# An attention and MLP kernel: value products and MLP behind six runs of scores a chunk, read out by VectorE

## The chip, the cores and the metric

The kernel runs on one core of a Trainium2 chip. A core has TensorE (matrix products into PSUM), VectorE, ScalarE (activations such as the exponential), GpSimd and SyncE, whose queue issues most DMAs. Each engine works through its own list of instructions in order, and waits on semaphores for the others. In profiles they are PE (PEld for TensorE's weight loads), ACT, DVE, POOL and SP.

The metric is the device time of one execution in microseconds. A comparison of two kernels is made over several executions on the same chip.

## The reference

One input of 2048 tokens by 640 features goes through two blocks in parallel, and their sum is added to it.

```python
xn = _layernorm(x)
# attention: 32 heads of 20 features
qkv = (xn @ wqkv) -> q, k, v          # each 32 x 2048 x 20
p = softmax(q @ k.T * 20 ** -0.5)
o = p @ v
A = o.reshape(2048, 640) @ wo
# MLP with a layernorm of its own, 640 -> 1536 -> 640, tanh GELU
y = _layernorm(xn)
B = gelu(y @ w1 + b1) @ w2 + b2
out = x + A + B
```

All inputs and the output are fp32. The kernel keeps the precision by splitting operands into two 16-bit halves and summing three partial products (the table `PASS`), or by fp32 products.

## The kernel before, in words

The first stage (up to about 217 us) normalizes, projects to q, k and v (lines 345 and 418), and prepares the weights of the MLP. The second stage does the attention and, in between on TensorE, the MLP. The third, short one projects the attention's output (the tile `z`, line 1156).

In the attention stage heads go in 16 pairs `g`, queries in two halves `hf` of 1024, and each half in two column blocks `cc` of 512. One such triple is called a chunk here; there are 64. A chunk goes over the 2048 keys in 16 key blocks of 128. For each key block:

- `scores` makes two matmuls (one per head of the pair, in two row tiles of TensorE, line 758) into a PSUM tile `s`, of which there are three, and ScalarE's exponential (line 760) turns it into an SBUF tile `p`, of which there are seven.
- For key blocks marked 1 in `SPLIT`, `rest` has VectorE compute `low`, the tile `p` less its upper 16 bits (line 772). There are four such buffers.
- `pv` multiplies with the values (line 789), in four column tiles of 32. A split key block takes four matmuls with the upper halves and two with `low`; a whole one takes two fp32 products. All of a chunk's products go into one PSUM tile `o`, of which there is one. The row sums of the softmax come out of the same products, through a column of ones beside the values.

After the last key block the sums are copied to SBUF (`ev`, line 810, ScalarE) and, after a chunk with `cc` = 1, sent to DRAM (`unload`). `finish` later divides by the row sums, piece by piece, on VectorE.

The MLP is a Python generator, `chain()`. It yields the cost of what it has just issued, in microseconds, and is asked for more whenever the attention has credit for it. `layer1` makes `pu` (30 matmuls of 256 columns, line 1041), followed by `gelu` on VectorE with one tanh on ScalarE (line 987); `layer2` makes `py` (36 matmuls of 320 columns, line 1071), followed by `addup` (line 1007). Both use the one PSUM buffer `m`. When the MLP is through, the chain goes on with the output projection `z`, as far as the attention's results are there.

The order of all engines' instructions is written out by hand (`manual_schedule`): the last loop of the kernel. Before the change it takes key blocks in groups of four: two scores, some MLP, two scores, then the value products of the group before. `tick()` moves each side job (GELU steps, finishing, loads of the next pair, which go to SP's queue) one step on. `rate` and `credit` say how much of the chain goes into each slot, 1.265 us four times a chunk; `CHUNK` bounds a piece.

The lines that set the order, in the words of the kernel:

```python
SPLIT = (1, 1, 0, 0) * (NKB // 4)
GRP = 4
...
                            rest(units[0])
                            credit += rate
                            other()
                        else:
                            for u in units[1:]:
                                rest(u)
                            if prev:
                                pv(prev)
```

Of the kernel before, what the change touches and what calls it, by code (L numbers as in the profile page):

```python
# [9 lines left out]
F32 = mybir.dt.float32  # L10
F16 = mybir.dt.float16
# [7 lines left out]
P = 128  # L19
# [12 lines left out]
QS = float(DH) ** -0.5 / 4.0  # L32
KROW = 32768.0
GRP = 4
CHUNK = 1.75
UNITS = (3, 3, 3, 3, 2, 2)
ENDS = tuple(sum(UNITS[: i + 1]) for i in range(len(UNITS)))
TAIL = 12
# [6 lines left out]
def mha_mlp_kernel(tc, x, wqkv, wo, w1, b1, w2, b2, out):  # L45
# [4 lines left out]
    with (  # L50
# [31 lines left out]
        ones = keep.tile([P, P], F32, name="ones")  # L82
# [21 lines left out]
        def pow2(acc, tag, total=None):  # L104

            lo = keep.tile([P, 1], F32, name=f"lo_{tag}")
            hi = keep.tile([P, 1], F32, name=f"hi_{tag}")
            if total is None:
                if tag == "k":
                    pt = psM.tile([P, 512], F32, tag="m", name="mxp")  # L110
                else:
                    pt = psS.tile([P, 2, 512], F32, tag="s", name="mxp")[:, 0, :]
                n = acc.shape[1]
                nc.tensor.matmul(pt[:, :n], ones, acc, start=True, stop=True)
# [12 lines left out]
            whole(lo, hi)  # L127
            return lo, hi
# [2 lines left out]
            nc.vector.tensor_scalar(lo, lo, 2.0**64, None, ALU.mult)  # L131
            exponents(lo, hi)

        pw, scales = {}, {}

        def split(pool, src, h, l, scale, n):

# [36 lines left out]

        with tc.tile_pool(name="pa", bufs=2) as pa, tc.tile_pool(name="pa1", bufs=1) as pa1, tc.manual_schedule():
            wv = pa1.tile([P, KD, 3, 2, D], F16, name="wv")

            stage = {}
            for n, t, i in (("q", w1t, 0), ("v", w1t, 1), ("k", w2t, 0)):
# [15 lines left out]
            nhalf = keep.tile([P, 4], F32, name="nhalf")  # L195
            half = keep.tile([H, 1], F32, name="half")
            nc.gpsimd.memset(ones, 1.0)
            nc.gpsimd.memset(nhalf, -0.5)
            eps = keep.tile([P, 1], F32, name="eps")
            nc.gpsimd.memset(eps, EPS)  # L200
# [87 lines left out]
            def factors_out():  # L288

                pr = psM.tile([P, 512], F32, tag="m", name="pr")[:NKB, :P]  # L290
                nc.tensor.transpose(pr, rall, ident)
                rrow = sm.tile([NKB, P], F32, tag="rrow", name="rrow", bufs=1)
                nc.vector.tensor_copy(rrow, pr)
                nc.gpsimd.dma_start(rscr, rrow)

# [382 lines left out]
        with ExitStack() as scope:  # L678
            pool = lambda **kw: scope.enter_context(tc.tile_pool(reuse_waits="tile", **kw))
            m0 = pool(name="m0", bufs=2)  # L680
            m1 = pool(name="m1", bufs=1)
            ptp = pool(name="pt", bufs=2 * GRP - 1)

# [83 lines left out]
            def rest(unit):  # L767

                kb, pt = unit[3:]
                if SPLIT[kb]:  # L770
                    low = ptp.tile([P, 2, 512], F16, tag="low", name="low", bufs=GRP)
                    nc.vector.tensor_sub(low, pt, upper(pt))  # L772
                    unit.append(low)

            evs = {}

            def pv(units):

                g, hf, cc, kb0 = units[0][:4]
                if kb0 == 0:
                    pv.o = psO.tile([P, 512], F32, tag="o", name="o")
                    pv.begun = set()
                last = units[-1][3] == NKB - 1

                def product(q, src, v0, t):
                    nc.tensor.matmul(pv.o[32 * q : 32 * q + 32, :], src[:, v0 - PAD * (1 - q % 2) :][:, :32], t,  # L789
                                     start=q not in pv.begun, stop=last, skip_group_check=True)  # L790
                    pv.begun.add(q)

                split = [(u[3], upper(u[4]), u[5]) for u in units if SPLIT[u[3]]]
                whole = [(u[3], u[4]) for u in units if not SPLIT[u[3]]]
                of16 = lambda kb, a: 2 * PAD + kb * 2 * VROW + (2 * g + a) * 2 * VW
                of32 = lambda kb, a: PAD + kb * VROW + (2 * g + a) * VW
                for kb, up, _ in split:
                    for a in range(2):
                        product(2 * a, vhalf, of16(kb, a), up[:, a])
                        product(2 * a + 1, vhalf, of16(kb, a) + VW, up[:, a])  # L800
                for a in range(2):
                    for n, (kb, _, low) in enumerate(split):
                        product(2 * a + n % 2, vhalf, of16(kb, a), low[:, a])
                for a in range(2):
                    for n, (kb, pt) in enumerate(whole):
                        product(2 * a + n % 2, vfull, of32(kb, a), pt[:, a])
                if last:
                    if cc == 0:
                        evs[g, hf] = m1.tile([P, 2, 512], F32, tag="ev", name="ev")
                    nc.scalar.activation(evs[g, hf][:, cc], pv.o, AF.Copy)  # L810
                    if cc == 1:
                        unload(g, hf, evs.pop((g, hf)))

            def dma(g, hf):

# [55 lines left out]
            def finish(g0, g1, hf):  # L871
# [16 lines left out]
                for c0 in range(0, 1024, w):  # L888
# [297 lines left out]
            with tc.manual_schedule():  # L1186
                fill = chain()
                sides.append(fetch_sums())
                credit = 0.0 - next(fill)
                rate = 1.265  # L1190
                groups = [(g, hf, cc, kb) for g, hf in ORDER for cc in range(2) for kb in range(0, NKB, GRP)]
                prev = None

                runs = []

                def other():

                    nonlocal credit
                    if not runs:
                        unit = next(fill)  # L1200
                        if unit is None:
                            credit = 0.0
                            return
                        n, cost = unit
                        k = max(round((cost - credit) / rate) + 1, math.ceil(cost / CHUNK))
                        runs.extend(n * (i + 1) // k - n * i // k for i in range(k))
                    for _ in range(runs.pop(0)):
                        credit -= next(fill)

                for g, hf, cc, kb0 in groups:  # L1210
                    units = []
                    for kb in range(kb0, kb0 + GRP):
                        units.append([g, hf, cc, kb, scores(g, hf, cc, kb)])
                        if kb % 2 == 0:
                            continue
                        reading[0] = kb % GRP > 1 and prev is not None and prev[-1][3] == NKB - 1
                        tick()
                        if kb % GRP == 1:

                            rest(units[0])
                            credit += rate
                            other()
                        else:
                            for u in units[1:]:
                                rest(u)
                            if prev:
                                pv(prev)
                            else:  # L1230

                                credit += rate
                                other()
                    prev = units
                    if cc == 0 and kb0 == 0 and (g, hf) != ORDER[-1]:
                        n = ORDER[ORDER.index((g, hf)) + 1]
                        sides.append(load_stack(*n, *([stacks[g, hf][1]] if n[0] == g else [])))
                n = 0
                reading[0] = False
                ended[0] = True  # L1240
# [25 lines left out]
def general(tc, nc, V, vscr, qkscr, oscr, accscr, gscale, ident, psS, psO, psM, project):  # L1266
# [2 lines left out]
    ds = bass.ds  # L1269
    nc.sync.dma_start(vscr, V)  # L1270

    assert SPLIT == (1, 1, 0, 0) * (NKB // 4)
    with (
        tc.tile_pool(name="g2", bufs=2) as g2,
        tc.For_i(0, S, P) as t,
# [1 line left out]
        with tc.For_i(0, D, DH) as r:  # L1277
# [10 lines left out]
            for b in range(2):  # L1288
                nc.vector.tensor_add(vt[:, b::4, :], vp[:, b::4, :DH], vp[:, b::4, VW : VW + DH])
# [63 lines left out]
```

## Time and profile before

| | us |
|---|---|
| median of three runs | 1332.44 (1332.02 to 1332.53) |
| the profiled execution | 1332.15 |
| its span, first to last instruction | 1330.2 |
| TensorE busy | 1323.6 (100%) |
| ScalarE busy | 1128.5 (85%) |
| VectorE busy | 1055.4 (79%) |
| first score starts | 216.8 |
| last score starts | 1262.7 |

Some ways of writing need a word. `o<-p,vfull` is an instruction that writes tile `o` from `p` and `vfull`. A row of the timeline gives start, duration, engine, line, operation, shape and how many equal instructions are merged. TensorE's matmuls overlap: one that lasts 0.39 us may be followed by the next after 0.22, so a rate is read from starts and not from durations. A row of groups gives busy time, the mean in ns of one, and the engine's idle time just ahead of it with what ended it. The granted clock of TensorE was 0.999 of full over the span.

### The profile page before, as it was taken

How to read it: one execution, taken by the hardware profiler on the slowest of the kernel's cores; microseconds unless marked ns; L12 is line 12 of the kernel's file. 1: busy time of each engine (PE TensorE's matmuls, PEld its weight loads, DVE VectorE, ACT ScalarE, POOL GpSimd, SP SyncE). 2: the span in 40 equal slices, each digit the busy share in tenths (PEclk: the TensorE clock that was granted, in tenths of full speed). 3: DMA queues.
4: the chain of work that ended last, by engine and by line, in shares of the span. 5: the costliest groups of instructions: out<-in, count | busy, mean ns of one | idle time of the engine just before them, and what ended most of it. 6: DMA issues, size and time to landing. Idle time of an engine off the chain costs nothing.

```text
span 1330.2 us, 29036 instructions
## 1 busy us (share of the span) xinstructions
PE 1323.6 (100%) x11636; PEld 586.9 (44%) x11636; DVE 1055.4 (79%) x1432; ACT 1128.5 (85%) x1306; POOL 34.9 (3%) x83
## 2 busy tenths in 40 slices
PE   9999999999999999999999999999999999999998
PEld 6645546443434343434344444334443434333366
DVE  7657845998788888879887888888878888997742
ACT  7844425999999999999999999999999999999900
POOL 2000000000000000000000000000000000000000
PEclk9999999999999999999999999999999999999999
DMA  8765532111122323122322032323032323334375
GB/s 283 254 214 174 146 103 59 34 56 41 49 67 63 88 57 95 49 63 52 114 75 69 23 102 59 89 61 90 20 80 72 95 64 88 119 101 117 102 221 187
DMA packets 100230, 129.54 MB, mean 97 GB/s; under 512 B 24180, under 2 KB 66568, under 8 KB 100092
## 3 DMA queue, kind: packets, MB, share of 16 engines
q1 hardware_dynamic: 96652, 120.25, 30.1%
q0 software_dynamic: 2816, 6.90, 2.8%
q8 instruction: 92, 1.51, 0.5%
q10 hardware_dynamic: 624, 0.51, 0.1%
q14 instruction: 46, 0.38, 0.1%
HBM read 82.14 MB, written 42.51 MB: 94 GB/s over the span
## 4 chain that ended last, share of the span: by engine, by line
PE 95%; DVE 3%; ACT 1%; issue 0%; DVEq 0%; POOL 0%; ACTq 0%; POOLq 0%
PE o L789 30%; PE s L758 20%; PE pu L1041 12%; PE py L1071 12%; PE qkp L345 10%; PE z L1156 5%; PE vp L418 5%; DVE low L772 2%; PE warm L235 1%; ACT p L760 1%; PE norms L390 0%; DVE w1t L730 0%; PE rb L941 0%; DVE wtmp L725 0%; PE pt L307 0%
## 5 line engine op out<-in xcount | busy, mean ns | idle before, releaser
L760 ACT ACTIVATE p<-s 128x1024 f32<-128x1024 f32 x1024 | 973.7, 1048 | 33.1 <-PE s L758 27.3
L772 DVE TENSOR_TENSOR low<-p 128x1024 f16<-128x1024 f32 x512 | 614.9, 1219 | 144.5 <-ACT p L760 143.7
L789 PE MATMUL o<-p,vfull 128*32 128x512 bf16 (+1 forms) x4096 | 429.0, 493 | 0.0
L758 PE MATMUL s<-qs,ks 61*128 61x512 f16 x2048 | 311.4, 381 | 0.2 <-ACT p L760 0.2
L758 PEld LDWEIGHTS <-ks 61*128 61x128 f16 x2048 | 61.2, 94 | 278.4 <-issue 276.4
L1071 PE MATMUL py<-w2t,hT 128*128 128x320 f16 x1152 | 178.5, 300 | 0.1
L1041 PE MATMUL pu<-xm,w1t 128*128 128x256 f16 x1440 | 178.2, 273 | 0.1
L1041 PEld LDWEIGHTS <-w1t 128*128 128x128 f16 x1440 | 131.0, 98 | 64.0 <-issue 50.2
L1071 PEld LDWEIGHTS <-hT 128*128 128x128 f16 x1152 | 102.3, 98 | 88.2 <-issue 53.9
L345 PE MATMUL qkp<-xnt,wv 128*128 128x512 f16 x600 | 131.2, 379 | 0.0
L789 PEld LDWEIGHTS <-vfull 128*32 128x32 f16 x3072 | 59.9, 95 | 138.4 <-issue 106.9
L789 PE MATMUL o<-low,vfull 128*32 128x512 f16 x1024 | 101.3, 377 | 0.1
L345 PEld LDWEIGHTS <-wv 128*128 128x128 f16 x600 | 58.3, 98 | 69.4 <-DVE wv L459 1.0
L789 PEld LDWEIGHTS o<-p,vfull 128*32 128x32 f32 x2048 | 61.7, 108 | 53.1
L1156 PE MATMUL z<-w1t,ot 128*128 128x320 f16 x480 | 67.4, 299 | 0.0
L418 PE MATMUL vp<-wv,xnt 128*128 128x320 f16 x480 | 66.8, 299 | 0.0
L360 ACT ACTIVATE qkhl<-qkp,qks 128x1024 f16<-128x1024 f32 (+1 forms) x24 | 23.2, 967 | 48.6 <-PE qkp L345 35.9
L1156 PEld LDWEIGHTS <-ot 128*128 128x128 f16 x480 | 46.0, 98 | 22.9 <-issue 5.5
L418 PEld LDWEIGHTS <-xnt 128*128 128x128 f16 x480 | 46.7, 98 | 18.5
L361 DVE SCALAR_TENSOR_TENSOR qkhl<-qkp,qks,qkhl 128x1024 f16<-128x1024 f32 (+1 forms) x24 | 26.5, 1105 | 28.3 <-ACT qkhl L360 28.2
L1113 DVE SCALAR_TENSOR_TENSOR acc<-z,sc,acc 128x320 f32<-128x320 f32 x32 | 17.5, 549 | 38.4 <-PE z L1156 38.1
L810 ACT ACTIVATE ev<-o 128x512 f32<-128x512 f32 x64 | 39.4, 615 | 2.3 <-PE o L789 2.2
(198 smaller groups left out, 670.9 us busy)
## 6 DMA issues: line engine op xcount, KB each, us to landing
qkscr<-qkhl SPq DMA_DIRECT2D x40, 256.0 KB
opart<-ev SPq DMA_DIRECT2D x124, 80.0 KB
ks<-qkscr SPq DMA_DIRECT2D x120, 80.0 KB
qs<-qkscr SPq DMA_DIRECT2D x192, 40.0 KB
oa<-opart SPq DMA_DIRECT2D x32, 240.0 KB
xt<-in_A_x_dram SPq DMA_DIRECT2D x16, 320.0 KB
xscr<-xnt SPq DMA_DIRECT2D x4, 1280.0 KB
xm<-xscr SPq DMA_DIRECT2D x8, 640.0 KB
```

Of the source, the lines that this page charges most:

```text
L345: nc.tensor.matmul(ps[:, i, :], wv[:, k, q, a, mm * P : (mm + 1) * P], xnts[c][:, k, b, :], start=(k + n == 0), stop=(k == KD - 1 and n == 2))
L360: nc.scalar.activation(hl[:, 0, i0:i1], ps[:, i0:i1], AF.Copy, scale=a)
L361: nc.vector.scalar_tensor_tensor(hl[:, 1, i0:i1], ps[:, i0:i1], a, hl[:, 0, i0:i1], ALU.mult, ALU.subtract)
L418: nc.tensor.matmul(ps[:, hf, :320], xnts[c][:, k, a, j * P : (j + 1) * P], wv[:, k, 2, b, hf * 320 : (hf + 1) * 320], start=(n == 0), stop ...
L758: nc.tensor.matmul(ps[:, a, :], ks[64 * a : 64 * a + 61, kb * P : (kb + 1) * P], qs[64 * a : 64 * a + 61, cc * 512 : (cc + 1) * 512], star ...
L760: nc.scalar.activation(pt, ps, AF.Exp, scale=QS)
L772: nc.vector.tensor_sub(low, pt, upper(pt))
L789: nc.tensor.matmul(pv.o[32 * q : 32 * q + 32, :], src[:, v0 - PAD * (1 - q % 2) :][:, :32], t, start=q not in pv.begun, stop=last, skip_gr ...
L810: nc.scalar.activation(evs[g, hf][:, cc], pv.o, AF.Copy)
L1041: nc.tensor.matmul(ps[:, i], w1v[:, k, (f + i) // 4, a, fo_ : fo_ + P], xnt[:, k, b, :], start=(n == 0), stop=(n == 3 * KD - 1))
L1071: nc.tensor.matmul(ps[:, :320], hTs[mc][:, f, a, j * P : (j + 1) * P], w2v[:, f, b, hf * 320 : (hf + 1) * 320], start=(n == 0), stop=(n == ...
L1156: nc.tensor.matmul(ps[:, :320], ot[:, k, a, j * P : (j + 1) * P], wov[:, k, b, h * 320 : (h + 1) * 320], start=(n == 0), stop=(n == 3 * KD ...
```

## The change

A table, `PLAN`, takes the place of the loop over groups. It has six rows for a chunk, and its words are done in order: `s` is the scores and exponential of the next key block, `v6` and `v4` the value products of the six or four oldest key blocks that still lack them, `m` a slot of the MLP, `l7` the lower half of key block 7, `t` and `r` a tick, `e` the read-out of the sums. Scores so come in runs of 3, 3, 2, 3, 3 and 2 key blocks; behind the runs stand value products and MLP in turn. The value products behind a chunk's first run are those of the last six key blocks of the chunk before.

`RATE` gives the three MLP slots of a chunk 1.6, 1.85 and 1.45 us. `SPLIT` still marks eight of 16 key blocks, but others. In `pv` the fp32 products now go first, in pairs of key blocks, then the upper halves, then the lower ones. The sums are read out by VectorE (line 818 of the changed kernel) in place of ScalarE. The numbers of buffers stay: seven `p`, four `low`, three `s`, one `o`. Besides, the constant `ones` and a small tile `rrow` move to a pool that ends with the first stage, and one late piece of `finish` loses its own buffer for `hl`.

```diff
-SPLIT = (1, 1, 0, 0) * (NKB // 4)
+SPLIT = (1, 1, 0, 0, 0, 0, 1, 1, 0, 0, 1, 1, 1, 1, 0, 0)
...
+RATE = (1.6, 1.85, 1.45)
+PLAN = ('s s s t v6 e', 's s s l0 l1 m t', 's s t v6 t', 's s s l6 t l7 t m', 's s s r l10 r l11 l12 v4', 's s l13 r m t')
...
-            ptp = pool(name="pt", bufs=2 * GRP - 1)
+            ptp = pool(name="pt", bufs=7)
...
-                    low = ptp.tile([P, 2, 512], F16, tag="low", name="low", bufs=GRP)
+                    low = ptp.tile([P, 2, 512], F16, tag="low", name="low", bufs=4)
...
+                for i in range(0, len(whole), 2):
+                    for a in range(2):
+                        for n, (kb, pt) in enumerate(whole[i : i + 2]):
+                            product(2 * a + n % 2, vfull, of32(kb, a), pt[:, a])
                 for kb, up, _ in split:
                     for a in range(2):
                         product(2 * a, vhalf, of16(kb, a), up[:, a])
                         product(2 * a + 1, vhalf, of16(kb, a) + VW, up[:, a])
-                for a in range(2):
-                    for n, (kb, _, low) in enumerate(split):
-                        product(2 * a + n % 2, vhalf, of16(kb, a), low[:, a])
-                for a in range(2):
-                    for n, (kb, pt) in enumerate(whole):
-                        product(2 * a + n % 2, vfull, of32(kb, a), pt[:, a])
+                for i in range(0, len(split), 2):
+                    for a in range(2):
+                        for n, (kb, _, low) in enumerate(split[i : i + 2]):
+                            product(2 * a + n % 2, vhalf, of16(kb, a), low[:, a])
...
-                    nc.scalar.activation(evs[g, hf][:, cc], pv.o, AF.Copy)
-                    if cc == 1:
-                        unload(g, hf, evs.pop((g, hf)))
+                    def out(o=pv.o):
+                        nc.vector.tensor_copy(evs[g, hf][:, cc], o)
+                        if cc == 1:
+                            unload(g, hf, evs.pop((g, hf)))
+
+                    if ended[0]:
+                        out()
+                    else:
+                        evict.append(out)
...
-                    if hf == 1 and TAIL < g1 and not last and c0 == 0:
-
-                        hl = m1.tile([P, D], F32, tag="xb", name="hl")[:, :512].bitcast(F16).rearrange(
-                            "p (s t) -> p s t", s=2)[: r1 - r0]
...
+                                now = int(step[1:])
+                                if prev[0] is units[0] and r == 0:
+                                    credit += RATE[0]
+                                    other(0)
+                                else:
+                                    pv(prev[:now])
+                                    del prev[:now]
+                        if cc == 0 and r == 1 and (g, hf) != ORDER[-1]:
+                            n = ORDER[ORDER.index((g, hf)) + 1]
+                            sides.append(load_stack(*n, *([stacks[g, hf][1]] if n[0] == g else [])))
```

What this does to the engines' lists is shown at three places. The first is TensorE's list at the end of a run of scores (`s`, from `qs` and `ks`) and the start of the value products (`o`, from `p` and the values `vfull`) in the middle of the attention stage. Before:

```order
L758 LDWEIGHTS ks_4660
L758 MATMUL s<-qs_5145,ks_4660 128x512
L789 LDWEIGHTS vfull
L789 MATMUL o<-p,vfull 32x512
L789 LDWEIGHTS vfull
L789 MATMUL o<-p,vfull 32x512
```

After, where the scores are those of a chunk's third key block:

```order
L761 LDWEIGHTS ks_4665
L761 MATMUL s<-qs_5158,ks_4665 128x512
L793 MATMUL o<-p,vfull 32x512 x4
L793 LDWEIGHTS vfull
L793 MATMUL o<-p,vfull 32x512
L793 LDWEIGHTS vfull
```

The fp32 products, which stand without a weight load of their own, have moved from the end of the value products to their start.

The second place is ScalarE's list over some chunks: exponentials `p<-s`, the read-out `ev<-o` and the tanh `w<-w`. Before:

```order
L760 ACTIVATE p<-s 128x1024 x8
L987 ACTIVATE w<-w 128x512
L760 ACTIVATE p<-s 128x1024 x8
L810 ACTIVATE ev<-o 128x512
L760 ACTIVATE p<-s 128x1024 x16
L810 ACTIVATE ev<-o 128x512
```

After:

```order
L763 ACTIVATE p<-s 128x1024 x26
L996 ACTIVATE w<-w 128x512
L763 ACTIVATE p<-s 128x1024 x24
L996 ACTIVATE w<-w 128x512
L763 ACTIVATE p<-s 128x1024 x14
L996 ACTIVATE w<-w 128x512
```

The read-out is gone from ScalarE's list, and 64 exponentials have three tanh among them.

The third place is VectorE's list in the same region: lower halves `low<-p`, the addition of an MLP result `xb`, finishing steps `oa`. Before:

```order
L772 TENSOR_TENSOR low<-p 128x1024
L964 CAST oa<-oa 120x512
L772 TENSOR_TENSOR low<-p 128x1024
L966 TENSOR_TENSOR oa<-oa 120x512
L772 TENSOR_TENSOR low<-p 128x1024 x2
L1007 SCALAR_TENSOR_TENSOR xb<-py,sc,xb 128x320
L772 TENSOR_TENSOR low<-p 128x1024 x4
```

After:

```order
L775 TENSOR_TENSOR low<-p 128x1024 x6
L1016 SCALAR_TENSOR_TENSOR xb<-py,sc,xb 128x320
L818 COPY ev<-o 128x512
L775 TENSOR_TENSOR low<-p 128x1024 x4
L985 TENSOR_TENSOR u<-pu,r2f 128x512
```

The read-out `ev<-o` stands here now, ahead of the lower halves of the new chunk.

More of the change, by code (lines that the diff above doesn't have):

```diff
@@ L113, in pow2 @@
                 n = acc.shape[1]
[L114 removed]
+                nc.tensor.matmul(pt[:, :n], ones_of[0], acc, start=True, stop=True)
                 nc.vector.tensor_reduce(lo, pt[:, :n], AX.X, ALU.add)
@@ L1204, in other @@
                         n, cost = unit
-                        k = max(round((cost - credit) / rate) + 1, math.ceil(cost / CHUNK))
-                        runs.extend(n * (i + 1) // k - n * i // k for i in range(k))
+                        lens, have = [], credit
+                        while not lens or (cost - have > 0.5 * RATE[(turn + len(lens)) % 3] and len(lens) < n):
+                            if lens:
+                                have += RATE[(turn + len(lens)) % 3]
+                            lens.append(max(0.0, have))
@@ L1207, in other @@
+                        cuts = [round(n * v / lens[-1]) for v in lens] if lens[-1] > 0 else [n]
+                        runs.extend(y - x for x, y in zip([0] + cuts, cuts))
                     for _ in range(runs.pop(0)):
                         credit -= next(fill)
-                for g, hf, cc, kb0 in groups:
+                for g, hf, cc in flow:
                     units = []
[L1212 to L1229, printed above, removed]
-                            else:
[L1232 to L1237, printed above, removed]
@@ new lines, in mha_mlp_kernel @@
+                    for r, steps in enumerate(PLAN):
+                        for step in steps.split():
+                            if step == "s":
+                                u = [g, hf, cc, len(units), scores(g, hf, cc, len(units))]
+                                units.append(u)
+                                prev.append(u)
+                            elif step in "tr":
+                                reading[0] = step == "r"
+                                tick()
+                            elif step == "m":
+                                credit += RATE[r // 2]
+                                other(r // 2)
+                            elif step == "e":
+                                if evict:
+                                    evict.pop()()
+                            elif step[0] == "l":
+                                if int(step[1:]) < len(units):
+                                    rest(units[int(step[1:])])
+                            else:
+                                now = int(step[1:])
[8 more added lines that the diff above has]
+                            sides.append(load_stack(*n, *([stacks[g, hf][1]] if n[0] == g else [])))
```

24 lines of the change are left out of this document (13 added, 11 removed).

## The prediction

> **What bounds the kernel now.** I read the page first: busy shares, the chain that ended last, the groups by cost.
>
> ```profile
> PE 1323.6 (100%) x11636; PEld 586.9 (44%) x11636; DVE 1055.4 (79%) x1432; ACT 1128.5 (85%) x1306; POOL 34.9 (3%) x83
> PE 95%; DVE 3%; ACT 1%; issue 0%; DVEq 0%; POOL 0%; ACTq 0%; POOLq 0%
> L760 ACT ACTIVATE p<-s 128x1024 f32<-128x1024 f32 x1024 | 973.7, 1048 | 33.1 <-PE s L758 27.3
> L758 PE MATMUL s<-qs,ks 61*128 61x512 f16 x2048 | 311.4, 381 | 0.2 <-ACT p L760 0.2
> L1071 PE MATMUL py<-w2t,hT 128*128 128x320 f16 x1152 | 178.5, 300 | 0.1
> L1041 PE MATMUL pu<-xm,w1t 128*128 128x256 f16 x1440 | 178.2, 273 | 0.1
> ```
>
> TensorE carries 95% of the chain. Over the whole span the scores waited 0.2 us for the exponentials, while the exponentials stood idle 27.3 us for scores. So TensorE leads and ScalarE follows, closely. Next the stage that the change rewrites, from the first score to the end of the last value products, by the windows view (the second and third row count the output projection, L1156, alone):
>
> ```profile
> 216.70:1266.00 1049.30, 1048.77 (x9822) 420.92 (x9824) 894.62 (x1065) 1015.11 (x1136) 14.39 (x17) 1.00 0.26 72
> ...
> 216.70:1266.00 1049.30, 11.52 (x72) 6.22 (x72) 1.00 0.26 72
> 1266.00:1330.20 64.20, 55.88 (x408) 39.76 (x408) 0.98 0.67 208
> ```
>
> The columns after the length are TensorE, weight loads, VectorE, ScalarE, GpSimd. In 1049.3 us TensorE is full, ScalarE works 1015.1 and VectorE 894.6. The stage has 64 chunks (16 head pairs, two halves, two column blocks), so 16.40 us a chunk. What fills TensorE there is shown by its timeline over two groups of four key blocks:
>
> ```profile
> 701.33 0.60 PE L758 MATMUL s<-qs,ks 61*128 61x512 f16 x4
> 701.86 1.81 PE L1041 MATMUL pu<-xm,w1t 128*128 128x256 f16 x15
> 703.61 0.60 PE L758 MATMUL s<-qs,ks 61*128 61x512 f16 x4
> ...
> 706.32 1.26 PE L1071 MATMUL py<-w2t,hT 128*128 128x320 f16 x8
> 707.52 0.61 PE L758 MATMUL s<-qs,ks 61*128 61x512 f16 x4
> 708.05 0.64 PE L789 MATMUL o<-p,vfull 128*32 128x512 bf16 x8
> 708.52 0.39 PE L789 MATMUL o<-low,vfull 128*32 128x512 f16 x4
> 708.74 1.03 PE L789 MATMUL o<-p,vfull 128*32 128x512 f32 x8
> 709.70 0.60 PE L758 MATMUL s<-qs,ks 61*128 61x512 f16 x4
> 710.23 1.53 PE L1071 MATMUL py<-w2t,hT 128*128 128x320 f16 x10
> 711.70 0.61 PE L758 MATMUL s<-qs,ks 61*128 61x512 f16 x4
> ```
>
> Read starts, not durations. Eight py matmuls take 1.20 us to the next run (706.32 to 707.52), ten take 1.47 (710.23 to 711.70): 0.135 each, and 0.12 stays for the run itself. By columns a pass of 512 is then 0.216. A score run of two key blocks takes 0.53: two passes (its two row tiles run together) and 0.10. A value run takes 1.65 (708.05 to 709.70): seven passes, four column tiles at a time (two for the upper halves, one for the lower, four for fp32, whose eight rows go four together), and 0.14. Fifteen pu take 1.75: 0.109 each and 0.12. So each run costs about 0.12 above its matmuls. The check: 8 x 0.53 + 4 x 1.65, fill (1440 x 0.109 + 1152 x 0.135 + 72 x 0.135) / 64 = 5.04, and 4 x 0.12 make 16.36, against 16.40 measured.
>
> The Trainium skill (TensorEngine Tiling (Array Packing), Key Properties) says that changing the tiling mode drains TensorE. That agrees with the 0.10 to 0.14; it gives no figure. The skill's single-matmul latency (TensorE: Matmul & The Clock Gate, Single matmul latency) has a constant of 166 ns; taken as the drain, an estimate, the gain below would be 42 us in place of 31 and the forecast 11 us lower; the rows bear out 0.12, so no chance is set on it.
>
> **The change, part by part.** I work against the profiled execution, 1332.15 us, 0.3 under the median.
>
> *Fewer runs.* A chunk goes from 8 score, 4 value and 4 MLP runs to 6, 3 and 3: 4 runs fewer, 4 x 0.12 x 64 = 31 us off TensorE. Matmuls are the same: 8 of 16 key blocks are still split.
>
> *Less fill.* The three budgets give 1.6 + 1.85 + 1.45 = 4.90 us a chunk where 5.04 went in. The MLP needs (1440 x 0.109 + 1152 x 0.135) / 64 = 4.88, so the 72 projection matmuls go behind the stage, where they cost 0.137 each by the chain's row: 9.9 us added to a tail which is dense on TensorE, and as much taken from the stage.
>
> ```profile
> 1267.33 9.48 PE z L1156 x69
> ```
>
> Dense, a new chunk is 16 x 0.216 + 6 x 0.10, 28 x 0.216 + 3 x 0.14, and 4.90 + 3 x 0.12: 15.8 us. Unhindered, the stage would lose 38 us and the tail gain 10.
>
> *What hinders it.* Buffers: seven for p, three for scores, in both kernels. After three scores of a new chunk the six last key blocks of the old one still wait for their value run. With key block 0 that is seven p tiles; the exponential of key block 1 cannot start before the value run has read one. The run now begins with the fp32 pair, so this is at the end of its first fp32 rows. In the trace of before, 27.3 of the exponentials' 33.1 us idle ended with scores and none with value products. The rows for a timetable:
>
> ```profile
> L758 PE MATMUL s<-qs,ks x2048: 372/386/388, 216.8 to 1262.7; 61*128 61x512 f16 x187
> L760 ACT ACTIVATE p<-s x1024: 1012/1032/1233, 217.5 to 1264.2; 128x1024 f32<-128x1024 f32 x171
> 701.76 1.94 ACT L760 ACTIVATE p<-s 128x1024 f32<-128x1024 f32 x2 [0.18 <-PE s L758]
> 706.22 3.77 ACT L760 ACTIVATE p<-s 128x1024 f32<-128x1024 f32 x4 [0.18 <-PE s L758]
> 709.85 0.65 ACT L987 ACTIVATE w<-w 128x512 f32<-128x512 f32 x1
> 710.37 3.79 ACT L760 ACTIVATE p<-s 128x1024 f32<-128x1024 f32 x4
> 714.02 0.63 ACT L810 ACTIVATE ev<-o 128x512 f32<-128x512 f32 x1
> 714.52 3.80 ACT L760 ACTIVATE p<-s 128x1024 f32<-128x1024 f32 x4
> ```
>
> An exponential starts 0.43 after its score (701.33 to 701.76), the next follows after 0.91 (706.22 to 709.85, four), its result is there after 1.03, and I let a waiter start 0.05 later (0.43 less the score's 0.386). fp32 rows are done 1.03 after their start. A tanh holds ScalarE 0.52, the read-out 0.50.
>
> Time 0 is a chunk's first score. Scores at 0, 0.22, 0.43; value run from 0.75. Exponential 0 at 0.43 frees ScalarE at 1.34, but 1 waits for 0.75 + 1.03 + 0.05 = 1.83: idle 0.49. 2 starts at 2.74, ends at 3.77. The value run has 10 passes, 2.30, so score 3 stands at 3.05 and score 5 could at 3.48; its PSUM needs exponential 2: **3.82, a wait of 0.34 in every chunk**. MLP from 4.14, score 6 at 5.86, second value run (11 passes, 2.52) from 6.39, score 8 at 8.91. Exponential 7 at 7.47, again behind fp32 rows; then ScalarE is dry until 9.34, since only two key blocks lie ahead of that long run: 0.96 idle. Score 13 needs exponential 10, 12.24 against 12.06: 0.18 waited. Third value run from 12.56, score 14 at 14.21, MLP from 14.75, the next chunk at 16.32. Exponential 15 starts at 15.71, so the next score 2 may go at 16.79 against 16.75 dense; each tanh that found no gap pushes that by 0.52, and 48 tanh in 64 chunks make 0.39.
>
> So a chunk takes 16.32 (every tanh in a gap) to 16.75 (none). I take 16.45, nearer the first, since two gaps of 0.5 and 1 stand open: 64 x 16.45 = 1053, 3.5 more than before, and 9.9 in the tail: 13 us, **1345**. The ends give -5 + 10 = 1337 and +23 + 10 = 1365.
>
> *Read-out on VectorE.* ScalarE loses 64 x 0.50 = 32 us. This buys only gaps: it is dry when scores are late. VectorE's price is not in the trace; the nearest rows read PSUM too:
>
> ```profile
> L976 DVE TENSOR_TENSOR u<-pu,r2f 128x512 f32<-128x512 f32 x48 | 32.9, 685 | 0.2
> L1007 DVE SCALAR_TENSOR_TENSOR xb<-py,sc,xb 128x320 f32<-128x320 f32 x32 | 17.5, 546 | 0.0
> L772 DVE TENSOR_TENSOR low<-p 128x1024 f16<-128x1024 f32 x512 | 614.9, 1219 | 144.5 <-ACT p L760 143.7
> ```
>
> 0.55 to 0.69, and I take 0.69, of equal width: 64 x 0.69 = 44 on 895 in 1053, 89%. It stands in VectorE's queue ahead of two lower halves and waits for the value run's end at 3.05. They are done by 3.74 + 2 x 1.22 = 6.2; the next value run wants the sums' PSUM at 6.39 and these halves at about 8.5. Covered, by 2.3 us; if VectorE is 3 us behind, it costs TensorE the difference. The lower half of key block 12 waits for the third value run (its buffers are four), with later GELU steps behind it: needed 4 us later, nothing.
>
> *Two more ticks a chunk* (10 for 8) step side jobs sooner after their DMAs on SP's queue; the read-out's six DMAs per half, on the same queue, follow VectorE in place of ScalarE, and the next pair's loads are asked for after six key blocks, not four, a chunk or more ahead of their use; GpSimd's queue keeps its order. Nothing on the path up to the last chunk. The end has six key blocks in the last value run for four, 0.65 later there and as much earlier above: nothing. The reused `hl` buffer in one late piece: nothing, for its result is read only in the tail. Constants moved between pools: nothing.
>
> **Rivals.** *The waits are smaller, TensorE stays dense.* For it: ScalarE has 34 us idle now and gets 32 more. It needs the first release before 1.3 us into the chunk, that is a value run whose first tile is read out 0.5 us sooner than its fp32 rows say. Then 1332 - 38 + 10 = 1304; with half of the 0.52 waited, 1320. The sign turns where waits fall under 28 / 64 = 0.44 a chunk. Against it: the 1.03 stands in a row and no buffer is free. The Trainium skill's warning (Perfetto Trace Analysis, Optimization Strategy) that equal gaps on an engine that should be full can mean too few buffers speaks for the forecast; no gap of the kind stands in this trace.
>
> *fp32 rows ahead of 16-bit rows cost a changeover, or VectorE falls behind.* Neither order stands in the trace; up to another 0.12 in three value runs is 23 us, and VectorE's waits come on top: 1358 to 1375.
>
> *Nothing measurable changes*: the waits come out at 0.40 to 0.48 a chunk instead of the 0.65 in my 16.45, and cancel the gain less the tail's 10.
>
> **How the numbers follow.** Forecast 0.62 (1337 to 1365, mostly under 1358), VectorE or changeover 0.11, TensorE dense or nearly 0.20 (1304 to 1329), no change 0.07. 0.2%, 2.7 us, is about what a measurement tells from no change. The range leaves out a tenth at each end: 1317 to 1361. Faster 0.20, same 0.07, slower 0.73.
>
> **What would show it.** Right: exponentials idle before value products some 0.5 us a chunk; scores waiting for exponentials some 30 us in all where it was 0.2; a stage of about 1053 us and a tail 10 longer with 480 projection matmuls; runs of 0.75 for three scores. Wrong: scores with no wait, a stage under 1030; or the value products waiting for the read-out.

## The result and the profile after

The changed kernel takes 1354.44 us, the median of six runs (1353.88 to 1356.55). The kernel before took 1332.54 beside it (1332.02 to 1332.77). The ratio is 1.0167, with a 95% interval of 1.0154 to 1.018: 22 us slower. The profiled execution took 1354.32 us, with a span of 1352.3.

The page of the changed kernel, its busy shares, its chain by engine, and the groups that answer to those shown of before (busy time and mean ns of one; then the idle time before them and what ended it):

```profile
PE 1323.2 (98%) x11636; PEld 635.1 (47%) x11636; DVE 1095.6 (81%) x1496; ACT 1098.6 (81%) x1242; POOL 35.4 (3%) x83
...
PE 80%; ACT 8%; issue 6%; DVE 5%; DMA 0%; SPq 0%; ACTq 0%; DVEq 0%
...
L763 ACT ACTIVATE p<-s 128x1024 f32<-128x1024 f32 x1024 | 964.8, 1043 | 69.5 <-PE s L761 38.2
...
L761 PE MATMUL s<-qs,ks 61*128 61x512 f16 x2048 | 314.4, 380 | 22.5 <-ACT p L763 21.0
...
L818 DVE COPY ev<-o 128x512 f32<-128x512 f32 x64 | 43.7, 683 | 43.8 <-PE o L793 43.8
```

TensorE's share of the chain fell from 95% to 80%, and its instructions are the same in number. The scores now wait 21.0 us for exponentials (0.2 before), and the exponentials stand idle 69.5 us (33.1 before). The view of waits says for what; after the name of the thing waited for come the total in us, the number of waits and the longest:

```profile
ACT p L763 <- PE s L761: 38.2, 85, 1.1
...
ACT p L763 <- PE o L793: 29.5, 83, 0.6
...
PE s L761 <- ACT p L763: 21.0, 83, 0.5
```

The second row is one that was not there before: an exponential that cannot start before value products have read a p tile. The windows view over the stage and the tail, parted at 1282.00, 0.35 us before the last value products are through; the second pair of rows counts the output projection alone:

```profile
217.10:1282.00 1064.90, 1042.41 (x9778) 465.11 (x9781) 931.92 (x1125) 985.88 (x1073) 14.87 (x18) 1.00 0.25 69
1282.00:1352.30 70.30, 65.56 (x500) 47.20 (x492) 24.00 (x48) 0.00 (x0) 0.67 (x2) 0.98 0.71 219
...
217.10:1282.00 1064.90, 3.03 (x21) 1.97 (x21) 1.00 0.25 69
1282.00:1352.30 70.30, 62.80 (x459) 44.75 (x459) 0.98 0.71 219
```

Counted from the first score to the first matmul behind the last value products, the stage went from 1050.5 to 1065.2 us, and the tail behind it from 63.0 to 69.9: 15 and 7 make the 22. From the starts of TensorE's instructions, each run counted from its first start to the next run's first start, the stage's 15 us is this sum:

| runs of the stage | before, us | after, us | difference |
|---|---|---|---|
| scores | 276.6 | 310.2 | +33.6 |
| value products | 423.1 | 417.7 | -5.4 |
| MLP | 340.0 | 334.4 | -5.6 |
| output projection | 10.8 | 3.0 | -7.8 |

Without a wait the new score runs would be 256 x 0.75 and 128 x 0.535, 260.5 us. So the scores' runs themselves save 16.1 and then wait 49.7. All gains of fewer runs are 16.1 + 5.4 + 5.6 = 27.1 us; the waits are nearly twice that. The view of waits has only 21.0 us of them, since it counts idle time from the listed end of the matmul before, and a listed matmul of 0.39 us hides the first part of each wait.

Where in a chunk they lie is seen in TensorE's timeline over one chunk, which begins at 715.83 (start, length, and in brackets the idle time ahead of the run). The 16 scores of a chunk are numbered from 0, and each is two instructions, one for either head:

```profile
715.83 0.82 PE L761 MATMUL s<-qs,ks 61*128 61x512 f16 x6
716.58 1.97 PE L793 MATMUL o<-p,vfull 128*32 128x512 f32 x24
718.37 0.61 PE L793 MATMUL o<-low,vfull 128*32 128x512 f16 x8
718.92 0.61 PE L761 MATMUL s<-qs,ks 61*128 61x512 f16 x4
719.75 0.39 PE L761 MATMUL s<-qs,ks 61*128 61x512 f16 x2 [0.23 <-ACT p L763]
720.07 1.48 PE L1050 MATMUL pu<-xm,w1t 128*128 128x256 f16 x12
...
727.37 0.96 PE L761 MATMUL s<-qs,ks 61*128 61x512 f16 x6
728.27 1.52 PE L793 MATMUL o<-p,vfull 128*32 128x512 f32 x16
```

The three-score run at 715.83 is dense, 0.75 to the next run. In the one at 718.92 the third score, score 5 of the chunk, starts 0.83 after the first, where 0.45 would be dense: 0.38 of waiting, and it is so in each of the 64 chunks. The run at 727.37 (scores 11 to 13) takes 0.90 to the next run, 0.15 too long. ScalarE over the same chunk:

```profile
716.29 1.02 ACT L763 ACTIVATE p<-s 128x1024 f32<-128x1024 f32 x1 [0.19 <-PE s L761]
717.76 6.52 ACT L763 ACTIVATE p<-s 128x1024 f32<-128x1024 f32 x7 [0.45 <-PE o L793]
725.04 7.45 ACT L763 ACTIVATE p<-s 128x1024 f32<-128x1024 f32 x8 [0.76 <-PE s L761]
```

Exponential 0 starts at 716.29. Exponential 1 finds no p tile until value products that began at 716.58 have read one, and starts at 717.76. Seven go back to back, and then ScalarE is dry for 0.76 before exponential 8.

Over all 64 chunks, the time by which a score starts later than the pass before it in its run lets it, by its place in the chunk (the table also has the experiments told below; us in total; the last column takes in the places not listed). The 49.7 above also holds what follows a run's last pass:

| kernel | score 2 | score 5 | score 7 | score 13 | all |
|---|---|---|---|---|---|
| after | 3.6 | 24.0 | 0 | 16.0 | 45.4 |
| upper halves first | 6.4 | 4.4 | 0 | 15.7 | 31.3 |
| eight p buffers | 4.5 | 1.7 | 1.6 | 18.5 | 30.1 |
| its control, seven | 3.4 | 23.1 | 0 | 16.0 | 44.3 |
| read-out on ScalarE | 3.7 | 24.6 | 9.8 | 16.0 | 55.3 |
| no tanh | 3.6 | 24.0 | 0 | 15.3 | 43.5 |
| six p buffers | 21.3 | 43.7 | 0 | 10.7 | 150.7 |

### The profile page after: what moved, and what is told of

Same layout as the page of the kernel before. It is cut to its first block, busy times and chain, and to the rows that moved or that the text cites. A ratio compares the mean times of both kernels' runs of the same rounds, so it can differ in the third digit from the quotient of the medians.

```text
span 1352.3 us, 29111 instructions
## 1 busy us (share of the span) xinstructions
PE 1323.2 (98%) x11636; PEld 635.1 (47%) x11636; DVE 1095.6 (81%) x1496; ACT 1098.6 (81%) x1242; POOL 35.4 (3%) x83
## 4 chain that ended last, share of the span: by engine, by line
PE 80%; ACT 8%; issue 6%; DVE 5%; DMA 0%; SPq 0%; ACTq 0%; DVEq 0%
PE o L793 23%; PE s L761 16%; PE py L1080 11%; PE qkp L348 10%; PE pu L1050 9%; ACT p L763 8%; PE vp L421 5%; PE z L1165 5%; DVE low L775 3%; DMA w1t<-in_A_wqkv_dram 0%; PE norms L393 0%; DVE oa L971 0%; DVE w1t L733 0%; PE rb L950 0%; PE pt L310 0%
## 5 line engine op out<-in xcount | busy, mean ns | idle before, releaser
L763 ACT ACTIVATE p<-s 128x1024 f32<-128x1024 f32 x1024 | 964.8, 1043 | 69.5 <-PE s L761 38.2
L775 DVE TENSOR_TENSOR low<-p 128x1024 f16<-128x1024 f32 x512 | 600.3, 1217 | 35.3 <-ACT p L763 34.7
L793 PE MATMUL o<-p,vfull 128*32 128x512 f32 (+1 forms) x4096 | 375.3, 495 | 0.0
L761 PEld LDWEIGHTS <-ks 61*128 61x128 f16 x2048 | 87.2, 94 | 222.0 <-issue 191.4
L1050 PE MATMUL pu<-xm,w1t 128*128 128x256 f16 x1440 | 173.9, 273 | 0.0
L1080 PE MATMUL py<-w2t,hT 128*128 128x320 f16 x1152 | 173.1, 300 | 0.0
L793 PEld LDWEIGHTS <-vfull 128*32 128x32 f16 x3072 | 90.9, 96 | 160.3 <-issue 117.2
L793 PEld LDWEIGHTS o<-p,vfull 128*32 128x32 f32 x2048 | 47.3, 108 | 97.3 <-issue 79.8
L793 PE MATMUL o<-low,vfull 128*32 128x512 f16 x1024 | 90.2, 377 | 0.0
L818 DVE COPY ev<-o 128x512 f32<-128x512 f32 x64 | 43.7, 683 | 43.8 <-PE o L793 43.8
L421 PEld LDWEIGHTS <-xnt 128*128 128x128 f16 x480 | 46.7, 98 | 18.5
```

The costliest lines, as they stand in the source:

```text
L421: nc.tensor.matmul(ps[:, hf, :320], xnts[c][:, k, a, j * P : (j + 1) * P], wv[:, k, 2, b, hf * 320 : (hf + 1) * 320], start=(n == 0), stop ...
L761: nc.tensor.matmul(ps[:, a, :], ks[64 * a : 64 * a + 61, kb * P : (kb + 1) * P], qs[64 * a : 64 * a + 61, cc * 512 : (cc + 1) * 512], star ...
L763: nc.scalar.activation(pt, ps, AF.Exp, scale=QS)
L818: nc.vector.tensor_copy(evs[g, hf][:, cc], o)
L1050: nc.tensor.matmul(ps[:, i], w1v[:, k, (f + i) // 4, a, fo_ : fo_ + P], xnt[:, k, b, :], start=(n == 0), stop=(n == 3 * KD - 1))
L1080: nc.tensor.matmul(ps[:, :320], hTs[mc][:, f, a, j * P : (j + 1) * P], w2v[:, f, b, hf * 320 : (hf + 1) * 320], start=(n == 0), stop=(n == ...
```

## The experiments

The theory: seven p tiles are held by the six last key blocks of the old chunk and the first of the new one; the value run's order (fp32 rows first) releases the first tile late; the late exponential 1 makes score 5 late through the three score buffers, and ScalarE running dry behind the run of two scores makes score 13 late. The rivals: it is the move of the read-out to VectorE, a changeover from fp32 to 16-bit rows inside a value run, or ScalarE's total load.

**Upper halves first.** The value run begins with the split key blocks' 16-bit upper halves, and the fp32 rows follow. The matmuls are the same.

```diff
-                for i in range(0, len(whole), 2):
-                    for a in range(2):
-                        for n, (kb, pt) in enumerate(whole[i : i + 2]):
-                            product(2 * a + n % 2, vfull, of32(kb, a), pt[:, a])
                 for kb, up, _ in split:
...
+                for i in range(0, len(whole), 2):
+                    for a in range(2):
+                        for n, (kb, pt) in enumerate(whole[i : i + 2]):
+                            product(2 * a + n % 2, vfull, of32(kb, a), pt[:, a])
```

> The changed kernel (1354.4 us, profiled span 1352.3) with the upper halves ahead of the fp32 products in each value run, as the kernel before had them; nothing else moves. Theory (the seven p buffers): the first release then comes 0.39 + 0.05 after the value run's start in place of 1.03 + 0.05, so the exponential of key block 1 may start at 1.2 us of the chunk and ScalarE is free only at 1.34: no idle time ahead of it. Score 5's wait, 24.0 us over the stage in the changed kernel, falls to 5 or less, the exponentials' idle time behind value products (29.5 us) to near 0; score 13's wait (16.0) stays. Part of it comes back as later waits: 1340 to 1348 us. Rival (VectorE is what is late): lower halves and read-out stand as before, so nothing changes, 1352 to 1356. Rival (the order of the products costs TensorE): the value runs of 2.33, 2.52 and 1.67 us get longer or shorter by 0.1, with score 5's wait as it is.

Measured: 1337.61 us, 1.0039 of before (1.0025 to 1.0053), 17 us under the changed kernel and a little more than expected.

```profile
L763 ACT ACTIVATE p<-s 128x1024 f32<-128x1024 f32 x1024 | 963.6, 1037 | 48.1 <-PE s L761 39.4 <-PE o L793 3.2 <-ACT p L763 0.9
L761 PE MATMUL s<-qs,ks 61*128 61x512 f16 x2048 | 308.0, 381 | 14.9 <-ACT p L763 11.7 <-ACT vfull L431 0.3
```

The exponentials' idle time behind value products falls from 29.5 to 3.2, and score 5's wait from 24.0 to 4.4. So, with seven p tiles, it is the order inside the value run that holds score 5. The profiled executions lie 15.5 us apart: score runs are 14.2 us shorter and value runs 2.0. The typical value run is 0.01 to 0.02 shorter in this order (1.645 for 1.666 in the run of 20 instructions, 2.504 for 2.524 in that of 28, 2.321 for 2.333 in that of 32); the kernel before, with fp32 rows last, has 1.644 in its runs of 20. That 0.02 is all that fp32 rows in front cost: the changeover rival asked for up to 0.12. Score 13's wait is left as it was.

**A control, and eight p buffers.** For an eighth p tile room has to be made. The control makes it by letting the reciprocals share the buffer of the second partial sum, so the addition of the two has to go ahead of their load, and all pieces but the first wait four more ticks for it; the next experiment adds the tile and nothing else.

```diff
-                        rb = m1.tile([P, 512], F32, tag="rb", name="rb")
+                        rb = o1
...
+                    if not last:
+                        if c0:
+                            yield from waits(4)
+                        nc.vector.tensor_add(o0, o0, o1)
...
-                    nc.vector.tensor_add(o0, o0, o1)
-                    yield
```

> The changed kernel, where finishing loads the reciprocal sums into the half of its operand tile that is free after the addition, in place of a tile of their own, and waits four more ticks for it. It frees 2 KB a partition and is the control for the next run. Seven p buffers stay. All theories: as the changed kernel, 1352 to 1359 us, with score 5 waiting some 24 us and score 13 some 16.

Measured: 1368.85 us, 1.0266 (1.0247 to 1.0285), 14 us above the changed kernel and more than expected. The exponentials, VectorE's waits and TensorE's, in the control:

```profile
L763 ACT ACTIVATE p<-s 128x1024 f32<-128x1024 f32 x1024 | 965.5, 1042 | 81.5 <-PE s L761 50.6 <-PE o L793 29.1
...
DVE oa L957 <- DMA oa<-opart: 21.7, 7, 4.6
...
PE pu L1052 <- DVE xb L1018: 6.2, 4, 1.8
PE o L793 <- DVE low L775: 5.0, 6, 1.6
```

The addition now stands in VectorE's queue before its data has landed, up to 4.6 us, and 21.7 us in all, where in the changed kernel VectorE waited 2.6 us for these loads; lower halves and MLP additions queue behind it, and TensorE waits 11.2 us for these. The waits of scores are those of the changed kernel (44.3 for 45.4). So the eighth tile is to be measured against this control.

```diff
-            ptp = pool(name="pt", bufs=7)
+            ptp = pool(name="pt", bufs=8)
```

> The control with eight p buffers, nothing else. Theory (seven p buffers): with eight the exponential of key block 1 has a free one; score 5's wait falls from 24 to 5 or less, the exponentials' idle time behind value products to near 0, and the time by 6 to 12 us against the control: 1341 to 1350. Score 13's wait (16) stays, since it comes from ScalarE running dry behind the run of two key blocks and the three score buffers. Rival (VectorE is late): no change against the control. Rival (all waits are the p buffers'): score 13's wait goes too, and the time falls to 1328 or less, under the kernel before.

Measured: 1357.01 us, 1.0187 (1.017 to 1.0204), 12 us under its control. That is the gain expected; the time expected had been reckoned without the 14 us that the control itself costs.

```profile
L763 ACT ACTIVATE p<-s 128x1024 f32<-128x1024 f32 x1024 | 961.6, 1034 | 67.8 <-PE s L761 66.8
```

No exponential is idle behind value products any more, and score 5's wait falls from 23.1 to 1.7 with the value run's order unchanged. Either remedy, an earlier first release or one more tile, takes away the same wait. Score 13's wait stays (18.5): an eighth p tile does not take it away.

**Six p buffers.** The same suspect in the other direction, on the changed kernel.

```diff
-            ptp = pool(name="pt", bufs=7)
+            ptp = pool(name="pt", bufs=6)
```

> The changed kernel with six p buffers. Theory: exponential 0 now has to wait for the first fp32 rows too, and 1 for the second release, as do those at each later value run; one exponential of 0.91 us is lost at each of the three value runs, up to 1.4 us a chunk: 1410 to 1450 us, with the waits of scores 4, 5 and 15 growing most. Rival (seven are enough and the waits are VectorE's or the score buffers'): 1352 to 1362.

Measured: 1461.74 us, 1.0974 (1.0956 to 1.0993), 107 us above the changed kernel and more than expected.

```profile
L763 ACT ACTIVATE p<-s 128x1024 f32<-128x1024 f32 x1024 | 965.8, 1032 | 179.9 <-PE o L793 176.3
L761 PE MATMUL s<-qs,ks 61*128 61x512 f16 x2048 | 348.3, 381 | 95.8 <-ACT p L763 89.9 <-ACT vfull L431 0.3
```

The score waits grow by 150.7 - 45.4 = 105 us, nearly the whole difference, and there are new ones (38.3 at score 4, 12.2 at 10, 23.1 at 15).

**Read-out back on ScalarE.** The changed kernel with the old engine for the read-out.

```diff
-                        nc.vector.tensor_copy(evs[g, hf][:, cc], o)
+                        nc.scalar.activation(evs[g, hf][:, cc], o, AF.Copy)
```

> The changed kernel with the read-out of the sums back on ScalarE, at the same place. Theory: ScalarE gets 64 x 0.50 = 32 us back and waits for the value run's end with exponentials queued behind it; VectorE, which has time to spare, gains nothing. Scores wait longer, by 10 to 20 us: 1362 to 1374. Rival (VectorE is what is late): the lower halves come sooner and the time falls, 1340 to 1352.

Measured: 1364.09 us, 1.0237 (1.022 to 1.0254), 10 us above the changed kernel, within what was expected. ScalarE's timeline at the start of a chunk, whose exponential 0 is at 719.46:

```profile
719.46 1.02 ACT L763 ACTIVATE p<-s 128x1024 f32<-128x1024 f32 x1 [0.19 <-PE s L761]
720.93 1.94 ACT L763 ACTIVATE p<-s 128x1024 f32<-128x1024 f32 x2 [0.45 <-PE o L793]
722.76 0.60 ACT L818 ACTIVATE ev<-o 128x512 f32<-128x512 f32 x1
723.23 4.71 ACT L763 ACTIVATE p<-s 128x1024 f32<-128x1024 f32 x5
```

The read-out stands between exponentials 2 and 3 and moves the later ones back by 0.47. Score 7, which had no wait, now waits 9.8 us, and the other two stay. So the move to VectorE is not the cause of the loss; in this order it saves 10 us.

**Read-out on VectorE in the kernel before.** That part of the change alone.

```diff
-                    nc.scalar.activation(evs[g, hf][:, cc], pv.o, AF.Copy)
+                    nc.vector.tensor_copy(evs[g, hf][:, cc], pv.o)
```

> The kernel before (1332.5 us) with the read-out on VectorE alone, at the same place of the order. Theory: the kernel before is bound by TensorE, and ScalarE's 32 us free nothing. The read-out stands on VectorE behind whatever is queued there and ahead of the next lower halves; the next chunk's first value run wants the sums' PSUM about 2.7 us later. Same or up to 10 us slower: 1331 to 1343. Rival (ScalarE is the hidden bound): faster, 1322 to 1329.

Measured: 1340.17 us, 1.0057 (1.0041 to 1.0074), 8 us slower. The exponentials and the value products:

```profile
L760 ACT ACTIVATE p<-s 128x1024 f32<-128x1024 f32 x1024 | 977.4, 1030 | 58.1 <-PE s L758 41.0 <-PE o L789 3.3 <-ACT p L760 1.5
...
L789 PE MATMUL o<-p,vfull 128*32 128x512 bf16 (+1 forms) x4096 | 428.6, 493 | 7.8 <-DVE ev L810 7.5
```

Here the value products do wait for VectorE's read-out, 7.5 us in 8 waits; in the changed kernel none is recorded. ScalarE's freed time turns into idle time (33.1 to 58.1). So the same part costs 8 us in the old order and saves 10 in the new one.

**No tanh.** The GELU's tanh is left out, so the MLP's values are others; ScalarE has 48 instructions fewer to do.

```diff
-                nc.scalar.activation(w, w, AF.Tanh, scale=0.7978845608028654 * 0.044715)
+                pass
```

> The changed kernel without the tanh of the GELU (the activation is left out, so the MLP's values are others; matmuls and VectorE work stay). Theory: 48 x 0.52 = 25 us less on ScalarE, most of it in gaps, so score 5's wait stays at 24 and only scores 13 and 2 wait less: 2 to 6 us faster, 1348 to 1352. Rival (ScalarE is the bound of the changed kernel): 15 to 25 us faster, 1330 to 1340.

Measured: 1352.75 us, 1.0158 (1.0141 to 1.0175), 2 us under the changed kernel, and the intervals overlap; the waits at scores 13 and 2, which were expected to fall, hardly do.

```profile
L763 ACT ACTIVATE p<-s 128x1024 f32<-128x1024 f32 x1024 | 961.4, 1045 | 98.0 <-PE s L761 58.7 <-PE o L793 38.9
```

ScalarE is relieved of 48 x 0.52 = 25 us, and its idle time grows from 69.5 to 98.0. Scores 2, 5 and 13 wait as before, so in the changed kernel the tanhs find their place in ScalarE's gaps. ScalarE's total load does not set the time; what it waits for at two places does.

**A larger fill.** The three budgets of MLP work are raised to 5.04 us a chunk, what the kernel before put in.

```diff
-RATE = (1.6, 1.85, 1.45)
+RATE = (1.65, 1.9, 1.49)
```

> The changed kernel with MLP slots of 1.65, 1.90 and 1.49 us, 5.04 a chunk, as much as the kernel before put in. Theory (the projection matmuls only change places): the tail loses some 7 to 10 us, the stage gains as much; 1350 to 1358. Other (longer slots give ScalarE time to catch up): waits of scores 5 and 13 fall, and the time to 1344 to 1350. Third (the slots fit the MLP's units badly, since 1.6 + 1.85 + 1.45 is just a second-layer unit of 4.9 and 5.04 is not): units end in mid-slot, chunks get uneven, 1360 to 1372.

Measured: 1374.25 us, 1.0312 (1.0295 to 1.0329), 20 us above the changed kernel and above all three ranges expected. The projection does return to the stage, and the tail falls from 70 to 62 us, but the stage grows by 28 (3 us of the profiled execution's span lie ahead of the stage, where nothing was changed).

```profile
L763 ACT ACTIVATE p<-s 128x1024 f32<-128x1024 f32 x1024 | 966.6, 1042 | 88.0 <-PE s L761 49.1 <-PE o L793 35.8
...
L761 PE MATMUL s<-qs,ks 61*128 61x512 f16 x2048 | 314.8, 380 | 33.0 <-ACT p L763 31.8 <-ACT vfull L431 0.3
...
L793 PE MATMUL o<-low,vfull 128*32 128x512 f16 x1024 | 94.0, 378 | 3.6 <-DVE low L775 3.5
```

With these budgets a slot takes now more and now fewer matmuls: pu runs of 9 to 30 where they were of 12, 15 and 18. The scores' waits rise to 55.4 us, the runs of 32 value instructions grow by 7, up to 4.13 us for 2.33, and the 8 us of projection come on top. It isn't told apart how much of the waiting comes from the uneven runs and how much from the longer chunk. So raising the budgets does not win back what the changed kernel loses; smaller ones were not run.

The uneven runs show what sets score 13's wait. Between scores 10 and 11 lies an MLP run (or, late in the stage, a projection run), and its length now varies. The chunks where exponential 8 starts as soon as score 8 is there (within 0.5 us of its start; 61 of 64 in the changed kernel, 55 here), by the length of that run:

| run between scores 10 and 11, us | chunks, changed kernel | chunks, larger fill | score 13's wait in each, us |
|---|---|---|---|
| 1.42 to 1.47 | 0 | 4 | 0.69 |
| 1.74 | 15 | 20 | 0.45 |
| 2.01 | 31 | 12 | 0.19 |
| 2.07 | 15 | 9 | 0.12 |
| 2.14 | 0 | 2 | 0.05 |
| 2.28 to 3.38 | 0 | 8 | 0 |

From 1.74 us on, the wait is 2.20 less the length of the run, and nothing beyond that. Score 13 needs the buffer that exponential 10 reads, and starts 0.05 after that one ends in all 64 chunks of the changed kernel; exponential 10 follows 8 back to back, and 8 could not start before score 8. So score 13 waits because of the three score buffers, behind a score 8 that came too late to keep ScalarE busy, and a run of 2.2 us or more in between hides the wait.

## Why the prediction was right in its direction and short in its size

The forecast of 1345 us (1317 to 1361) held the 1354.44, and slower was its likeliest case. The loss was 22 us for the 13 predicted. By its own steps:

- *Fewer runs*: 31 us at 0.12 a run; the runs show 27.1. A score run saved 0.126, an MLP run 0.10, a value run only 0.08. The value runs that stayed are up to 0.02 longer, some 3 us in all, for fp32 rows ahead of 16-bit rows, which the prediction had kept apart as a rival; that rival's larger cost did not come.
- *Less fill*: 480 projection matmuls behind the stage; there were 459, 51 more than before and not 72. The tail grew by 7.0 us, not 9.9, and the stage lost 7.8. Between the two it was worth 1 us.
- *What hinders it*, exponential 1: forecast 1.83 us into the chunk and 1.40 after exponential 0. The chunk shown has 1.93 (715.83 to 717.76) and 1.47; the release came 1.18 after the first value product for the 1.08 forecast. Right, and shown by three experiments (the order, a tile more, a tile fewer).
- *What hinders it*, score 5: 0.34 in every chunk forecast, 0.38 in every chunk measured. Score 13: 0.18 forecast, 16.0 / 64 = 0.25 measured. Score 2: up to 0.43, put down to tanhs; 3.6 us in all, and 3.6 without the tanh, so the tanh is not what it waits for.
- *The mis-sized term*: "I take 16.45", a stage of 1053 us; it took 1065, 16.64 a chunk, inside the 16.32 to 16.75 given for it. The waits came to 49.7 us where 0.65 x 64 = 42 was taken, 8 more, and without them the stage would take 1015 for the 15.8 x 64 = 1011 reckoned, 4 more. These 12 us, less the 3 of the tail, are the 9 between 13 and 22. The mechanism was right, but the 42 was put together otherwise than the 49.7. It held 33 us of waits at scores 5 and 13 and 8 us for tanhs without a gap. Scores 5 and 13 waited 40, the other scores 5.4, and 4.3 lie behind the last pass of a run, where nothing was forecast. The tanhs cost next to nothing: the score waits are 45.4 us with them and 43.5 without. That the forecast missed by 9 us and not by 17 is in part luck, since the term for the tanhs covered for waits that were set too small.
- *Read-out on VectorE*: 0.69 us forecast, 0.683 measured. "Covered": no value product waits for it in the changed kernel. "This buys only gaps" was wrong: in the new order the way back costs 10 us, at score 7.
- *TensorE stays dense*: no. The score waits are there. Even with upper halves first, and 14 us less of them, the kernel stands 5 us above the one before.

The Trainium skill's remark (Perfetto Trace Analysis, Optimization Strategy) that a gap which repeats on the engine that should be full can come from too few buffers agrees with the runs: on TensorE score 5 waits 0.38 us in every chunk with seven p tiles, 23.1 us over the control's stage, and with eight tiles 1.7 us.

Score 13's wait is about the same with another value order, an eighth tile, the read-out on either engine, and without the tanh. The prediction's timetable puts it down to ScalarE running dry behind the run of two scores and to the three score buffers, and the table by run length bears that out. The timetable has an MLP run of 1.97 us there, and in the mean they are 1.96; the 0.25 measured for 0.18 comes in the main from exponential 8, which starts 0.49 after its score where 0.43 was taken.

What stays open: no run had a fourth score buffer, or the run lengths set so that score 13 never waits and nothing else moves. Nor was an eighth p tile tried without the control's shared buffer, or together with the other order. No version run is faster than the kernel before; the nearest is 5 us behind.

## What to carry to other kernels

Before a regrouping that saves changeovers, count the tiles that the pending work holds at the moment the next producer needs one, and order the consumer so that its first release comes early: here the same matmuls in another order were worth 17 us, one buffer more 12 us, and one fewer cost 107. Where a late result frees a buffer, the filling work placed ahead of its next user can hide the wait, if the piece is long enough: here 2.2 us. Price a step that moves between engines in the order it will stand in, since the same read-out cost 8 us in one order and saved 10 in the other. When a buffer is shared to make room, look at what the reordered step waits for, because everything behind it on its engine's queue waits too.

## What the runs showed of the hardware that I had not expected

- fp32 rows ahead of 16-bit rows in one run cost 0.01 to 0.02 us a run (1.666 for 1.645, 2.524 for 2.504, 2.333 for 2.321), far under the 0.08 to 0.13 saved for each run of another kind that fell away.
- One instruction on VectorE whose data came by DMA up to 4.6 us late, seven times in all, was followed by a kernel 14 us slower.
